# Inverse-root store and broadcast issued by GpSimd, and k^T v computed in two groups of head pairs per batch

## Chip, cores and metric

The kernel runs on one core of a Trainium2 chip. The metric is the device time of one execution in microseconds; the median of three runs is compared.

## What is computed

A linear attention without softmax, then two feed-forward blocks, all in float32 (reference, cut):

```python
kv  = np.einsum('bhsd,bhse->bhde', k, v)        # 8 batches, 8 heads, 576 rows, head size 64
out = np.einsum('bhsd,bhde->bhse', q, kv)
rms = np.sqrt(np.mean(out * out, axis=-1, keepdims=True) + 1e-06)
x   = (out / rms * g_norm)                       # then (4608, 512)
r   = np.maximum(x @ w_in, 0.0)                  # w_in 512 x 2048, w_out 2048 x 512
x   = (s * (r * r) + b) @ w_out
h   = x @ w2_in
out = (h * (1.0 / (1.0 + np.exp(-1.702 * h)))) @ w2_out
```

## The kernel before

**Tiling.** The 4608 tokens are nine token blocks of 512. A batch has 576 tokens, so block j holds the end of batch j-1 and the beginning of batch j. Activations lie transposed (features on partitions). A float32 product is made of three passes over a high and a low part of each operand, so one feed-forward step of 128 features takes twelve 128x128x512 matmuls. The first feed-forward of blocks 0 to 2 is plain (`plain`); later blocks are worked in pairs with seven products in place of eight (`first_products`, `second_plain`, `second_products`). During block 0 the weights of the first feed-forward are decoded from 64-bit words on the fly (`w_low`, `w_words`, `w_hi`, `w_lo`), a weight unit per step, by ScalarE and VectorE.

**What sets the order.** There is no scheduler: `at(slot, fn, ...)` enters a call with a slot number, the list is sorted by slot, and every engine's instructions are issued in that order. A slot is one step of twelve wide matmuls; block j of the plain stage begins at slot 32 j, so blocks 0 to 2 are slots 0 to 95. Each engine, and each queue that issues transfers, is in order: an instruction that waits holds back all behind it. SyncE (SP) issues all transfers, and each of its issues also waits for the one eight issues earlier to have landed (eight counting semaphores, used in turn). Buffers come from rings (`Slots`), 23 of 128x512 (`mid`), 42 twice as wide (`big`), 8 PSUM banks; a new tile waits for the last reader of the buffer that has been free longest.

**k^T v.** For each batch b, `kv_load` (L275) brings k and v of one head pair (two transfers of 256 KB), `tail_load` (L278, L280) the last 64 rows, `kv_product` (L311, L315) makes the 64x64 products of all four head pairs in one go (64 short passes and 8 tail passes), and `kv_keep` (L323) copies them to SBUF. The table `KV` gives the slot of the product for batches 1 to 7; the loads are entered 3.3 to 1.8 slots ahead, the tail 1.3 ahead. Batch 0 is done at the start, pair by pair.

**Attention of block j** (`attend`): q loads (L293), the products (L342), squares and copies, one mean over the heads (L396), then ln/exp and a Newton step (L369, L370) give the inverse root y for eight heads. `y_store` (L411) writes the eight rows of y to DRAM, `y_load` (L417) reads each row back broadcast to 64 partitions, two transfers per head pair, eight in all; `att_scale` (L422, VectorE) multiplies; `att_split` splits into high and low part, or from block 3 on stores to DRAM (`x0d`, L429). Both y steps stand on SP.

Of the kernel before, what the change touches and what calls it, by code (L numbers as in the profile page):

```python
# [10 lines left out]
AF = mybir.ActivationFunctionType  # L11
ALU = mybir.AluOpType

P = 128
T = 512
B, H, S, D = 8, 8, 576, 64
DM, DFF = 512, 2048
NP = H // 2
NG = NP // 2
# [6 lines left out]


START = [(-61, -60, -54, -52, -45), (-59, -54, -53, -47, -42), (-54, -48, -48, -43, -41), (-50, -49, -46, -40, -36)]
KV = (1, 29, 34, 64.6, 80, 86, 92)
CONV = [(0, 1, 2, 3), (-0.5, 0, 1, 1.5)]  # L30


# [31 lines left out]
def kernel(ctx: ExitStack, tc: tile.TileContext, q_h, kv_h, kt, vt, cst,  # L64
# [6 lines left out]
    nc = tc.nc  # L71
    pe, act, dve, pool = nc.tensor, nc.scalar, nc.vector, nc.gpsimd
# [13 lines left out]
    def drop(*tiles):  # L86
        for t in tiles:
            slots, n, _ = where.pop(id(t))
            slots.give(n)
# [4 lines left out]
    def new2(dtype, name):  # L94
        return new(mid, [P, T], dtype, name)

    def psum(name):
        return new(bank, [P, T], F32, name)
# [10 lines left out]
    kvs = [cp.tile([P, NG, 2, D], F32, name=f"kvs{i}") for i in range(4)]  # L109
# [158 lines left out]
    kvin, kvp, qin, xT, done = {}, {}, {}, {}, set()  # L268
    xd = [[dp.tile([NP, P, T], F32, name=f"x{m}d{j}") for j in range(NB)] for m in range(2)]
    yd = [dp.tile([H, T], F32, name=f"yd{j}") for j in range(NB)]  # L270
# [31 lines left out]
    def kv_product(b, units, first, last):  # L302
        if first:
            kvp[b] = psum("kv")
        kv = kvp[b].rearrange("q (g c) -> q g c", g=NP)
        for h in range(2):
            for c in range(4):
                for p in units:
                    r, o = p % 2 * D, c * P + h * D
                    kt_, vt_ = (t[:, o:o + D] for t in kvin[b, p])  # L310
                    pe.matmul(kv[r:r + D, p // 2, h * D:(h + 1) * D], lhsT=kt_, rhs=vt_, start=(p < 2 and h == 0 and c == 0), stop=False,  # L311
                              skip_group_check=True)
        for p in units:
            r = p % 2 * D
            pe.matmul(kv[r:r + D, p // 2, :], lhsT=tail_k[:, p // 2, p % 2, :], rhs=tail_v[:, p // 2, p % 2, :],  # L315
                      start=False, stop=True, skip_group_check=True)
            drop(*kvin.pop((b, p)))

    def kv_keep(b, p):
        r = p % 2 * D  # L320
        src = kvp[b].rearrange("q (g h c) -> q g h c", g=NP, h=2)
        if b:
            act.activation(kvs[b % 4], src[:, 0:NG], AF.Copy)  # L323
            done.update(("kv", b, n) for n in range(NP))
            drop(kvp.pop(b))
            return
        act.activation(kvs[0][r:r + D, p // 2], src[r:r + D, p // 2], AF.Copy)
        done.add(("kv", b, p))
        if p == NP - 1:
            drop(kvp.pop(b))  # L330
# [77 lines left out]

    def y_store(j):
        y = att.pop(j)  # L410
        nc.sync.dma_start(out=yd[j], in_=y[0:P:P // H])  # L411
        drop(y)

    def y_load(j, p):
        y = new2(F32, "yb")
        for h in range(2):
            nc.sync.dma_start(out=y[h * D:(h + 1) * D], in_=yd[j][2 * p + h:2 * p + h + 1].to_broadcast([D, T]))  # L417
        att[j, p] = (att[j, p][0], y)

    def att_scale(j, p):  # L420
# [312 lines left out]
    def at(slot, fn, *a):  # L733
        events.append((slot, len(events), fn, a))
# [11 lines left out]
    def attend(j, slot, gap, late):  # L746
        for g in range(NG):
            at(slot - 4 + g, q_load, j, g)
            at(slot + gap * g, att_product, j, (2 * g, 2 * g + 1))
            for r in range(2):  # L750
                at(slot + gap * g + 0.4 + 0.3 * r, att_square, j, 2 * g + r)
                at(slot + gap * g + 0.4 + 0.3 * r, att_copy, j, 2 * g + r)
        slot += gap + 1.4
        at(slot, block_mean, j)
        at(slot + 0.5, block_root, j)
        at(slot + 1.2, block_newton, j)
        at(slot + 1.8, y_store, j)
        for p in range(NP):
            at(slot + 2.7, y_load, j, p)
            at(slot + late + 1.1 * p, att_scale, j, p)  # L760
            at(slot + late + 1.1 * p + 0.3, att_split, j, p)

# [114 lines left out]
    for p in range(NP):  # L877
        at(-99 + p, kv_load, 0, p)
        if p == 0:
            at(-98.95, tail_load, 0)  # L880
        at(START[p][0], kv_product, 0, (p,), p == 0, p == NP - 1)
        at(START[p][0], kv_keep, 0, p)
        at(-98.9 + p, q_half, p)
        o, m, n, x = START[p][1:]
        attention((o, m, m, n, x), 0, p)
# [5 lines left out]
        weight(n - (5 if n < 12 else 4), n - 1, 1, CONV[1], 0, f, w)  # L891


    for b, slot in zip(range(1, B), KV):
        for p in range(NP):
            at(slot - 3.3 + 0.5 * p, kv_load, b, p)
        at(slot - 1.3, tail_load, b)
        at(slot, kv_product, b, range(NP), True, True)
        at(slot + 0.5, kv_keep, b, 0)


    for j in range(NPLAIN):
# [14 lines left out]
    for j, slot in zip(range(1, NPLAIN + 2), (10, 35.5, 49, 66)):  # L917
        attend(j, slot, 4, 4.8)
    for j in range(NPLAIN, NB - 2, 2):
        for n, slot in enumerate((5, 16) if j == NPLAIN else (0.5, 12)):  # L920
            attend(j + 2 + n, firsts[0, j] + slot, 4, 4.8)
# [14 lines left out]
    for k in range(2):  # L936
        slot = seconds[1, NB - 3] + 10 + 4 * k
# [10 lines left out]
    for i in range(NF // 2):  # L948
        slot = 50 + 5.4 * i
# [10 lines left out]
    slot = 32 * NPLAIN + 4  # L960
# [64 lines left out]
```

## Time and profile before

| | us |
|---|---|
| median of three runs | 1581.72 (1580.92 to 1583.14) |
| the profiled execution's own time | 1583.73 |
| its span in the trace | 1581.9 |
| TensorE (PE) busy | 1538.5 (97%) |
| VectorE (DVE) busy | 1063.5 (67%) |
| ScalarE (ACT) busy | 793.4 (50%) |
| GpSimd (POOL) busy | 1.6 (12 instructions) |
| transfers, share of 16 DMA engines | 70.3% |

Times are counted from the start of the span. The shares are averages over stages with different limits: the start (to about 37 us), block 0 with the decoding of weights (to about 143), blocks 1 and 2 (to about 360), and then the paired blocks. TensorE's busy time grows when its granted clock falls, so a busy PE is not always PE at its full rate. A row of a timeline gives start, duration, engine, line, operation, and in brackets the idle time before it with what ended that.

### The profile page before, as it was taken

The page shows a single profiled execution, that of the slowest core. Times are in us where ns is not written, and L with a number is a line of the kernel's source. Part 1 is how long each engine was busy: PE and PEld are TensorE (multiplying, and loading weights), DVE is VectorE, ACT ScalarE, POOL GpSimd, SP SyncE. Part 2 cuts the span into 40 slices and gives each one's busy share as a digit, 9 for nine tenths or more (in the row PEclk, how much of TensorE's full clock was granted, in tenths as well). Part 3 has the DMA queues.
Part 4 walks back from the last instruction along what each step waited for, and adds up shares of the span by engine and source line. Part 5 has one row for each costly group of instructions (what it writes and reads, how often), then busy time and mean ns, then how long its engine had stood idle before and what let it go on. Part 6 is the DMA issues. An engine that isn't in the chain of part 4 may idle for free.

```text
span 1581.9 us, 20440 instructions
## 1 busy us (share of the span) xinstructions
PE 1538.5 (97%) x7316; PEld 1238.8 (78%) x7316; DVE 1063.5 (67%) x1535; ACT 793.4 (50%) x1162; POOL 1.6 (0%) x12
## 2 busy tenths in 40 slices
PE   7988998999899999999999999999999999999999
PEld 4766776787688877888888888888888888888887
DVE  4996463565679477866672579867967796688422
ACT  4987453454598357944692225423532452234222
POOL 0000000000000000000000000000000000000000
PEclk8999999999999999999999999999999999999999
DMA  9535547779899688959870866885788478746680
GB/s 303 190 121 187 202 160 283 259 266 319 267 333 336 214 316 334 379 187 339 332 297 16 303 223 239 273 300 199 264 287 301 171 271 281 259 139 206 223 311 27
DMA packets 177444, 392.09 MB, mean 248 GB/s; under 512 B 22912, under 2 KB 54656, under 8 KB 177344
## 3 DMA queue, kind: packets, MB, share of 16 engines
q1 hardware_dynamic: 177344, 390.80, 70.3%
q8 instruction: 58, 0.95, 0.2%
q14 instruction: 42, 0.34, 0.1%
HBM read 300.42 MB, written 90.31 MB: 247 GB/s over the span
## 4 chain that ended last, share of the span: by engine, by line
PE 84%; DMA 6%; DVE 5%; ACT 2%; SPq 1%; issue 1%; DVEq 0%; ACTq 0%
PE o L523 25%; PE o L694 19%; PE d L566 9%; PE a L566 9%; PE h L480 7%; PE b L566 4%; PE f L566 4%; PE c L566 4%; DMA v_in<-in_kv 2%; DMA raw<-in_w_in 2%; DVE cu L157 1%; PE o_ps L342 1%; PE kv L311 1%; DVE ca L158 1%; DMA x0d<-oc 1%
## 5 line engine op out<-in xcount | busy, mean ns | idle before, releaser
L523 PE MATMUL o<-gh,w 128*128 128x512 f32 x1280 | 407.3, 391 | 2.0 <-DVE w L173 0.8
L523 PEld LDWEIGHTS o<-gh,w 128*128 128x128 f32 x1280 | 239.8, 188 | 59.4 <-DVE w L173 3.6
L694 PE MATMUL o<-gh,wl 128*128 128x512 f32 x896 | 276.4, 389 | 0.0
L523 PE MATMUL o<-gl,w 128*128 128x512 f32 x640 | 249.9, 391 | 0.4 <-DVE gl L513 0.2
L694 PEld LDWEIGHTS o<-gh,wl 128*128 128x128 f32 x896 | 168.2, 188 | 34.9
L480 PE MATMUL h<-xh,w 128*128 128x512 f32 x512 | 171.9, 397 | 7.0 <-DVE w L173 3.3
L694 PE MATMUL o<-gl,wl 128*128 128x512 f32 x448 | 174.3, 389 | 0.0
L566 PE MATMUL d<-xh,wl 128*128 128x512 f32 x448 | 157.9, 393 | 5.7 <-DVE r L592 5.7
L566 PE MATMUL a<-xh,wl 128*128 128x512 f32 x448 | 157.6, 393 | 1.0 <-DMA wl<-wsd 1.0
L523 PEld LDWEIGHTS o<-gl,w 128*128 128x128 f32 x640 | 120.3, 188 | 26.9 <-DVE gl L513 2.4
L480 PEld LDWEIGHTS h<-xh,w 128*128 128x128 f32 x512 | 96.6, 190 | 35.6 <-DVE w L173 6.8
L582 ACT ACTIVATE c<-a 128x512 f32<-128x512 f32 x56 | 33.5, 597 | 168.0 <-PE a L566 165.0
L566 PEld LDWEIGHTS d<-xh,wl 128*128 128x128 f32 x448 | 84.6, 189 | 25.9 <-DVE r L592 7.4
L566 PEld LDWEIGHTS a<-xh,wl 128*128 128x128 f32 x448 | 84.6, 189 | 21.9 <-issue 1.9
L480 PE MATMUL h<-xl,w 128*128 128x512 f32 x256 | 100.7, 393 | 0.2 <-DVE xl L442 0.2
L694 PEld LDWEIGHTS o<-gl,wl 128*128 128x128 f32 x448 | 84.1, 188 | 17.5
L637 DVE TENSOR_TENSOR gl<-r,gh 128x512 fp32r<-128x512 f32 x96 | 65.1, 687 | 40.5 <-PE o L523 23.4
L566 PE MATMUL d<-xl,wl 128*128 128x512 f32 x224 | 87.6, 391 | 0.0
L566 PE MATMUL a<-xl,wl 128*128 128x512 f32 x224 | 87.6, 391 | 0.0
L668 ACT ACTIVATE gh<-t 128x1024 fp32r<-128x1024 f32 x48 | 51.0, 1062 | 72.5 <-DVE t L659 60.6
L621 ACT ACTIVATE r<-r 128x1024 f32<-128x1024 f32 x84 | 84.6, 1054 | 0.0
L673 DVE TENSOR_TENSOR gl<-r,gh 128x1024 fp32r<-128x1024 f32 x64 | 77.1, 1218 | 6.9 <-ACT gh L668 6.9
(114 smaller groups left out, 2483.7 us busy)
## 6 DMA issues: line engine op xcount, KB each, us to landing
wl<-wsd SPq DMA_DIRECT2D x168, 512.0 KB, 6.7
wl<-wo2S SPq DMA_DIRECT2D x64, 512.0 KB, 5.4
wsd<-op SPq DMA_DIRECT2D x96, 256.0 KB, 4.1
w<-wod SPq DMA_DIRECT2D x48, 512.0 KB, 7.8
wl<-wo2A SPq DMA_DIRECT2D x48, 512.0 KB, 4.6
raw<-in_w_in SPq DMA_DIRECT2D x32, 512.0 KB, 7.1
raw<-in_w_out SPq DMA_DIRECT2D x32, 512.0 KB, 8.6
wl<-wsd SPq DMA_DIRECT2D x56, 256.0 KB, 5.8
```

The costliest lines, as they stand in the source:

```text
L157: dve.scalar_tensor_tensor(out=t, in0=raw[:, :, 1], scalar=SIGN_TOP, in1=t, op0=ALU.bitwise_and, op1=ALU.bitwise_or)
L158: dve.tensor_tensor(out=q, in0=t, in1=q, op=ALU.add)
L311: pe.matmul(kv[r:r + D, p // 2, h * D:(h + 1) * D], lhsT=kt_, rhs=vt_, start=(p < 2 and h == 0 and c == 0), stop=False, skip_group_check=True)
L480: pe.matmul(h, lhsT=a, rhs=b, start=(n == 0), stop=(n == 3 * NP - 1))
L523: pe.matmul(acc[m, j][c], lhsT=a, rhs=x, start=(f == 0 and n == 0), stop=(f == NF - 1 and n == 2))
L566: pe.matmul(o, lhsT=a, rhs=b, start=(first and n == 0), stop=(n == 5), skip_group_check=not first)
L582: act.activation(st["c1"], st[0], AF.Copy)
L621: act.activation(R[q, n], R[q, n], fn)
L637: dve.tensor_sub(out=gl, in0=R[q, i][:, half, :], in1=gh.bitcast(F32))
L668: act.activation(hi, src, AF.Copy)
L673: dve.tensor_sub(out=lo, in0=src, in1=hi.bitcast(F32))
L694: pe.matmul(so[k, d], lhsT=a, rhs=b, start=(first and n == 0 and i == 0 and e == 0), stop=(n == 3 and i == 1 and e == 2), skip_group_check ...
```

## The change

`y_store` and `y_load` are issued by GpSimd. The eight transfers of `y_load` are entered from 2.6 slots after the mean's slot on, pair by pair 0.9 slots apart, where all stood at 2.7. The products of k and v are made in two groups of two head pairs, each with a slot of its own; a group's loads are entered 5.5 and 4.8 slots ahead, the tail 4 slots ahead of the first group. The accumulation's first-write flag is set per group, and each group is copied to SBUF by itself, so the copy is half as wide and there are two per batch. One PSUM bank holds a batch's products from its first group to its second.

```diff
-KV = (1, 29, 34, 64.6, 80, 86, 92)
+KV = ((1, 5), (20, 27), (34, 41), (46, 57), (62.5, 66.5), (74, 79), (84, 89))
...
+        opens = units[0] if b else 0
...
-                    pe.matmul(kv[r:r + D, p // 2, h * D:(h + 1) * D], lhsT=kt_, rhs=vt_, start=(p < 2 and h == 0 and c == 0), stop=False,
+                    pe.matmul(kv[r:r + D, p // 2, h * D:(h + 1) * D], lhsT=kt_, rhs=vt_, start=(p in (opens, opens + 1) and h == 0 and c == 0), stop=False,
...
-            act.activation(kvs[b % 4], src[:, 0:NG], AF.Copy)
-            done.update(("kv", b, n) for n in range(NP))
+            act.activation(kvs[b % 4][:, p // 2], src[:, p // 2], AF.Copy)
+            done.update((("kv", b, p), ("kv", b, p + 1)))
...
     def y_store(j):
         y = att.pop(j)
-        nc.sync.dma_start(out=yd[j], in_=y[0:P:P // H])
+        pool.dma_start(out=yd[j], in_=y[0:P:P // H])
...
-            nc.sync.dma_start(out=y[h * D:(h + 1) * D], in_=yd[j][2 * p + h:2 * p + h + 1].to_broadcast([D, T]))
+            pool.dma_start(out=y[h * D:(h + 1) * D], in_=yd[j][2 * p + h:2 * p + h + 1].to_broadcast([D, T]))
...
-            at(slot + 2.7, y_load, j, p)
+            at(slot + 2.6 + 0.9 * p, y_load, j, p)
...
-    for b, slot in zip(range(1, B), KV):
-        for p in range(NP):
-            at(slot - 3.3 + 0.5 * p, kv_load, b, p)
-        at(slot - 1.3, tail_load, b)
-        at(slot, kv_product, b, range(NP), True, True)
-        at(slot + 0.5, kv_keep, b, 0)
+    for b, slots in zip(range(1, B), KV):
+        for g, slot in enumerate(slots):
+            for r in range(2):
+                at(slot - 5.5 + 0.7 * r, kv_load, b, 2 * g + r)
+            if g == 0:
+                at(slot - 4, tail_load, b)
+            at(slot, kv_product, b, (2 * g, 2 * g + 1), True, True)
+            at(slot + 0.6, kv_keep, b, 2 * g)
```

Three places in the order of instructions. From L304 on the changed kernel's line numbers are one higher.

SP in block 0, around the y store of block 1 (`raw` are weight units, `yd` and `yb` the store and the broadcast of y), before:

```order
L138 DMA raw_1003<-in_w1_out 128x1024
L411 DMA yd1_139<-y_949 8x512
L133 DMA raw_1035<-in_w1_in 128x4x256
L417 DMA yb_1037<-yd1_139 64x512 x2
L417 DMA yb_1040<-yd1_139 64x512 x2
L417 DMA yb_1043<-yd1_139 64x512 x2
L417 DMA yb_1046<-yd1_139 64x512 x2
L138 DMA raw_1075<-in_w1_out 128x1024
```

and with the change:

```order
L133 DMA raw_888<-in_w1_in 128x4x256
L275 DMA k_in_909<-in_kv 128x512
L275 DMA v_in_910<-in_kv 128x512
L138 DMA raw_938<-in_w1_out 128x1024
L275 DMA k_in_945<-in_kv 128x512
L275 DMA v_in_946<-in_kv 128x512
L133 DMA raw_983<-in_w1_in 128x4x256
L278 DMA tail_k_78<-in_kt 128x256
L280 DMA tail_v_79<-in_vt 64x4x64 x2
L138 DMA raw_1016<-in_w1_out 128x1024
L133 DMA raw_1048<-in_w1_in 128x4x256
```

The store and the eight broadcasts left SP, and the loads of batch 2's first group came in at about the same place.

TensorE around the product of batch 4, before:

```order
L480 MATMUL h<-xl,w 128x512
L480 MATMUL h<-xh,w 128x512
L311 MATMUL kv<-v_in,k_in 64x64 x32
L315 MATMUL kv<-tail_v,tail_k 64x128 x4
L523 MATMUL o<-gh,w 128x512
```

and the second group of batch 4 with the change (the first stands 11 slots ahead of it, and both ahead of that place):

```order
L481 MATMUL h<-xh,w 128x512
L312 MATMUL kv<-v_in,k_in 64x64 x16
L316 MATMUL kv<-tail_v,tail_k 64x128 x2
L524 MATMUL o<-gh,w 128x512
L524 MATMUL o<-gl,w 128x512
```

The run of short matmuls is halved and stands in two places.

SP in the paired stage, around the broadcast of block 5 (`wl` are weights for TensorE, `x0d` the store of the scaled block), before:

```order
L417 DMA yb<-yd_143 64x512 x8
L243 DMA wsd_0_104<-op 128x512 x2
L254 DMA wl<-wsd_4_100 128x1024
L254 DMA wl<-wsd_4_100 128x512
L254 DMA wl<-wsd_5_101 128x1024
L429 DMA x0d_125<-oc 128x512
```

and with the change:

```order
L293 DMA qq<-in_q 128x128
L243 DMA wsd_0_104<-op 128x512 x2
L254 DMA wl<-wsd_4_100 128x1024
L254 DMA wl<-wsd_4_100 128x512
L254 DMA wl<-wsd_5_101 128x1024
L430 DMA x0d_125<-oc 128x512
```

The eight broadcasts ahead of the weight loads are gone from SP; they stand on GpSimd's queue, which holds nothing else after its first memsets.

## Rows read from the trace of the kernel before

**Rows 1.** The page's head.

```profile
span 1581.9 us, 20440 instructions
```

**Rows 2.** TensorE's waits, whole span: total us, times, longest us.

```profile
PE kv L311 <- DMA v_in<-in_kv: 12.5, 8, 2.6
PE d L566 <- DVE r L592: 5.7, 4, 2.9
...
PE h L480 <- DVE w L173: 3.3, 2, 2.0
...
PE a L566 <- DMA wl<-wsd: 1.0, 1, 1.0
```

**Rows 3.** Stretches around products: length, PE, PEld, DVE, ACT, POOL, PEclk, DMA, GB/s.

```profile
243.80:256.50 12.70, 4.91 (x74) 4.25 (x73) 3.73 (x6) 2.42 (x4) 0.00 (x0) 0.73 0.97 339
303.90:311.30 7.40, 4.09 (x74) 3.48 (x73) 0.15 (x1) 0.00 (x0) 0.00 (x0) 0.84 0.92 295
328.30:332.30 4.00, 2.86 (x74) 2.52 (x73) 0.00 (x0) 0.00 (x0) 0.00 (x0) 1.00 1.06 378
...
135.55:138.10 2.55, 2.55 (x74) 2.38 (x73) 2.45 (x6) 2.52 (x5) 0.00 (x0) 1.00 0.02 6
```

**Rows 4.** Chain of waits after batch 2's product: start, us, what.

```profile
138.08 2.99 PE h L480 x12
141.06 2.72 PE o L523 x12
```

**Rows 5.** SP's issues ahead of batch 4's product.

```profile
225.04 4.94 SPq L417 DMA_DIRECT2D yb<-yd  x8
...
246.52 0.44 SPq L275 DMA_DIRECT2D v_in<-in_kv  x1
```

**Rows 6.** Stages in block 0 and block 2, columns as in Rows 3.

```profile
60.00:80.00 20.00, 19.60 (x105) 13.44 (x104) 19.32 (x35) 18.50 (x33) 0.00 (x0) 1.00 0.46 166
...
300.00:350.00 50.00, 45.55 (x346) 37.39 (x346) 26.20 (x41) 21.40 (x32) 0.00 (x0) 0.97 0.85 293
```

**Rows 7.** VectorE's timeline in block 0.

```profile
96.75 0.69 DVE L370 SCALAR_TENSOR_TENSOR y<-y,y 128x512 f32<-128x512 f32 x1
...
109.38 0.75 DVE L422 SCALAR_TENSOR_TENSOR oc<-oc,g_col,yb 128x512 f32<-128x512 f32 x1
...
124.47 0.74 DVE L422 SCALAR_TENSOR_TENSOR oc<-oc,g_col,yb 128x512 f32<-128x512 f32 x1
...
135.19 0.68 DVE L173 TENSOR_TENSOR w<-ca,w 128x512 fp32r<-128x512 f32 x1
```

**Rows 8.** SP's issues around the broadcast of block 5.

```profile
398.32 0.60 SPq L411 DMA_DIRECT2D yd<-y  x1
...
402.39 6.34 SPq L417 DMA_DIRECT2D yb<-yd  x8
...
409.88 1.67 SPq L254 DMA_DIRECT2D wl<-wsd  x3
411.65 0.38 SPq L429 DMA_DIRECT2D x0d<-oc  x1
```

**Rows 9.** Chain of waits behind that.

```profile
422.20 2.92 PE d L566 x6
425.12 2.56 PE a L566 x6
```

**Rows 10.** Line L417, all 64 broadcasts: issue ns min/median/max, and landing.

```profile
L417 SPq DMA_DIRECT2D yb<-yd x64: 444/587/1253, 99.3 to 615.5; - x64
...
DMA to landing us min/median/max: 2.8/3.1/6.0
```

**Rows 11.** ScalarE's copy of one batch's products: duration ns min/median/max.

```profile
L323 ACT ACTIVATE kvs<-kv x7: 368/385/387, 46.0 to 351.4; 128x256 f32<-128x256 f32 x7
```

**Rows 12.** VectorE's groups from 97 to 125 us: busy us, mean ns.

```profile
L173 DVE TENSOR_TENSOR w<-ca,w 128x512 fp32r<-128x512 f32 x7 | 4.8, 682 | 0.0
L152 DVE TENSOR_SCALAR cu<-cu 128x512 uint32<-128x512 uint32 x7 | 3.0, 427 | 0.2
```

## The prediction

> **What bounds it now.** I read the head of the page first: the span is 1581.9 us [rows 1], the profiled execution took 1583.73, the median of the runs is 1581.72. So the sum below is made against 1583.73, and 2.0 us come off at the end. TensorE is busy 97% of the span (the table above), so the change can gain only where TensorE waits, or where its granted clock is low because it has just waited.
>
> Then TensorE's waits [rows 2]. The largest that the change touches is `kv` on `v_in`: 12.5 us in 8 waits, 2.6 at the longest. The reader is to see that one batch's product waits several times, once for each head pair whose load is late. `d` on `r` (5.7) and `h` on the weight word `w` (3.3) come next; `a` on `wl` is a single 1.0.
>
> Then the stretches around single products [rows 3]. The product of batch 2 is the undisturbed one: 2.55 us for its 74 matmuls, clock 1.00. Batch 4's took 12.70 us at a granted clock of 0.73, batch 5's 7.40 at 0.84, batch 6's 4.00 at 1.00. In these three the transfers were busy at 0.97, 0.92 and 1.06 of the 16 engines, against 0.02 in the first. So the loads, entered only 3.3 slots ahead, compete with the rest and are late. For batch 4 something else adds: the issues on SP. The eight broadcasts of y took SP 4.94 us from 225.04 on, and the last `v_in` went out at 246.52, after the product had begun to wait [rows 5].
>
> Then block 0. There DVE is busy 19.32 us of 20 and TensorE 19.60 [rows 6]: weights are decoded as they are used, and DVE sets the pace. TensorE's wait for `w` [rows 2] belongs here.
>
> Last, the broadcast of block 5 [rows 8]: eight issues from 402.39 for 6.34 us, the three loads of `wl` at 409.88 and the store `x0d` at 411.65, behind them on the same queue. The chain that ended last then shows six `d` in 2.92 us and six `a` in 2.56 [rows 9], where twelve matmuls at full clock take 2.72 [rows 4], so six take 1.36.
>
> **The change part by part.**
>
> *Loads ahead, two groups (batches 4, 5, 6).* Undisturbed, three products are 3 x 2.55 = 7.65 us; they took 12.70 + 7.40 + 4.00 = 24.10 [rows 3]. At most 16.45 us are to be had. A slot is twelve matmuls, 2.72 us, so 5.5 slots are 15 us, against 9 before; a group needs two pairs (1 MB) in place of four; and the eight broadcasts are not ahead of the loads on SP any more. I take the whole. Against that, a product is a run of small matmuls, and the twelve matmuls after batch 2's took 2.99 us, against 2.72 later [rows 4]: 0.27 us for each break. Five batches (3 to 7) are broken once more each: 1.35 us. **-16.45 + 1.35 = -15.1.** Bounds: -17 (the breaks cost nothing), and -8 if half of the loads stay late.
>
> *Batch 2.* Its product moves from slot 29 to 20 and 27, and the copy with it. At 135.55 it stood just ahead of a wait: `w` was ready at 135.19 + 0.68 = 135.87 [rows 7], and the next `h` began at 138.08 [rows 4]. So 2.2 us of the 2.55 were TensorE's own delay there; at the new slots the product lies in waits that TensorE has anyway, because DVE sets the pace. **-2**, bounds 0 and -2.8 (2.55 + 0.27).
>
> *SP without y (block 5).* The 6.34 us leave SP ahead of `wl` and `x0d`. Gone with them: the wait of `a` on `wl`, 1.0; one of `d` on `r`, 2.9, since the late `x0d` holds a buffer for which DVE waits, and DVE's `r` behind it [rows 2]; the slow clock after them, (2.92 - 1.36) + (2.56 - 1.36) = 2.76 [rows 4, 9]. Together 6.7; that the `x0d` store is behind the wait of `d` I infer from the order alone, so I take **-5**, bounds 0 and -6.7. The Trainium skill speaks against this term ("DMA: Bandwidth & Descriptors", section "Issuing engines are not separate DMA queues"): all issuers share the same 16 engines, and a second issuer saves only the time of issuing, usually small beside the transfer. By that rule the sum would be 5 us poorer; here the issuing itself is 6.34 us [rows 8], so I go by the row.
>
> In block 0 SP's freedom brings nothing: DVE sets the pace [rows 6], and word loads that go out sooner wait for it.
>
> *The copies.* One more `kvs` copy per batch on ScalarE, at most 0.385 us each [rows 11], and half as wide; seven are 2.7 at most. Most lie beside TensorE's work; three fall in block 0, where ScalarE is at 18.50 of 20 [rows 6]. **+0.5**, bounds 0 and 1.2.
>
> *The price X of an issue by GpSimd.* No row of before shows one. The nearest are SP's issues of the same transfers: 0.44 us shortest, 0.587 median, 1.25 longest; landing 2.8 to 6.0 us, median 3.1 [rows 10]. GpSimd can be cheaper than SP's shortest or dearer than its longest; nothing excludes either. I take X = 1.25, the dear end. GpSimd holds nothing else, so what queues behind its waits is only y itself. Who waits is DVE's `att_scale`. In block 0, y is done at 96.75 + 0.69 = 97.44 [rows 7]; store issue and landing 1.25 + 3.1, first pair 2.5 + 3.1: ready at 107.4, while its scale began at 109.38 [rows 7]; each later pair comes 2.5 us after, and the last scale began at 124.47 against 114.9. So it hides. In the paired stage DVE has room. **+0.5** for a scale that comes a little late there, bounds 0 and (rival below) much more.
>
> *Sum:* -15.1 - 2 - 5 + 0.5 + 0.5 = -21.1. 1583.73 - 21.1 = 1562.6 for a profiled execution, less 2.0: **1560** for the median, rounded down from 1560.6.
>
> **Rivals.**
>
> *The loads stay late in part.* The stretches already show 0.92 to 1.06 of the transfers' capacity [rows 3], and a load entered sooner only stands sooner in a full queue; it may also wait on SP for a buffer. Against it: over 300 to 350 the share is 0.85 [rows 6], so there is room outside the bursts. Half of the first term gone (+7.5), and half of the third (+2.5), leaves -11: **1571**.
>
> *GpSimd's issues are slow, and the scale waits: slower.* DVE is in order, so an `att_scale` that waits for `yb` holds all decoding behind it, in the stage where DVE sets the pace. Pair p is there at 97.44 + X + 3.1 + 2X(p+1) + 3.1. At X = 4 the first is there at 115.6 (109.38 is needed) and the last at 139.6 (124.47 is needed): 15 us late, all of it in the time. In the four paired-stage broadcasts up to block 8 the same lateness of 15 us reaches TensorE by half, as DVE has slack there: some 30. With -21 that is +24: **1606**. It decides from X = 3.1: there the last pair of block 0 is 7 us late and half of 7 at the four others makes 14, together the 21 gained. What speaks for it: DVE's units here take 427 ns and 682 ns for tiles of one size [rows 12], so some run in a faster form, and DVE leaves no gap [rows 6]. Against it: no row shows GpSimd issuing. The Trainium skill has a rule by which it would go this way ("SBUF — State Buffer", section "SBUF: two separate sides"): transfers issued by GpSimd need descriptors that it writes through a port shared with DVE, and DVE's fast forms lock it out. The page's figure is 620 ns alone and some 3100 beside a copy by DVE; by that estimate the gain would be just about eaten (1582).
>
> *It does nothing that can be told.* A measurement of this kernel tells some 0.2%, 3.2 us, from no change. Gain and lateness would have to cancel within that: X close to 3.1 with the loads in time.
>
> **How the numbers follow.** The forecast has 0.62. Late loads 0.23: the full queues are in the rows, the room beside them too. Slow issues 0.12: a fast form of DVE is in the rows, but between two of its instructions GpSimd can get in. Nothing 0.03. Faster by over 0.2% is the forecast and the late loads: 0.85; same 0.03; slower 0.12. The range: all upper bounds together (-17 - 2.8 - 6.7) give 1583.73 - 2.0 - 26.5 = 1555, a little less if waits that I haven't named go too, so 1551; above, late loads with 5 us of new waits, or an X between 2 and 3, 1576. Some 0.18 lies outside.
>
> **What would show it.** In the changed profile TensorE should no longer wait for `v_in`; each group of a product should take about 1.3 us at a clock of 1.00; the waits of `a` and `d` near block 5's broadcast should be gone, with its six matmuls at 1.36; the `yb` transfers should land ahead of every `att_scale` of block 0. The second group of batch 2 should no longer hold back an `h` whose `w` is ready. I am wrong if DVE's scale waits for `yb` in block 0 or if the landing of `yb` on GpSimd's queue takes over 6 us (slow issues); if `kv` still waits for `v_in` or `k_in` with the transfers at 0.9 or more (late loads); or if the waits that go are made up by others, on `r` or on `wl`, in the paired stage.

## The result, and the profile after

The changed kernel takes **1565.2 us** (median of four runs, 1564.6 to 1566.29) against 1582.43 for the kernel before beside it: ratio 0.9891, 95% interval 0.9874 to 0.9908, so 17.2 us less. The forecast was 1560, which is 21.7 less than the 1581.72 it started from. The profiled executions differ by 19.1 us: that of before was 1.3 above its median here, that of the change 0.6 below. Medians and ratios below leave out one execution of one kernel (number 11), which took 3108.3 us.

One sentence ahead of the prediction is to be corrected: a batch's products don't hold one PSUM bank from the first group to the second. Each group takes a bank of its own and gives it back with its copy (`first` is true for both, and `kv_keep` drops the bank each time). No step of the prediction rests on it.

The page's head, and TensorE's waits in the changed kernel (total us, times, longest), which answer to [rows 1, 2]:

```profile
span 1562.8 us, 20560 instructions
```

```profile
PE d L567 <- DVE r L593: 7.0, 6, 2.0
...
PE kv L312 <- DMA v_in<-in_kv: 2.3, 2, 1.2
...
PE h L481 <- DVE w L173: 0.4, 1, 0.4
```

(`a` and `d` are matmuls of the paired blocks; `d` reads `r`, which VectorE writes.) `v_in` went from 12.5 to 2.3, and what is left lies in the start, where batch 0 is worked as before (1.5 of the 12.5 lay there). The wait for `w` went from 3.3 to 0.4, that of `a` on `wl` is gone. The wait of `d` on `r` rose from 5.7 to 7.0. A group of a product, with the wide matmuls at its edges (the two groups of batch 5, columns as in [rows 3]), now reads:

```profile
239.03:240.57 1.54, 1.54 (x38) 1.37 (x38) 0.96 (x2) 1.51 (x3) 0.00 (x0) 1.00 0.91 311
252.47:254.00 1.53, 1.53 (x41) 1.36 (x38) 0.78 (x2) 1.41 (x3) 0.00 (x0) 1.00 1.07 415
```

The clock is at 1.00 beside transfers at 0.91 and 1.07: here full transfers don't slow a product whose operands are there. The whole batch takes 3.07 us, where it took 7.40.

The step of twelve matmuls behind a group is slower, as it was behind one piece. Here are the steps ahead of and behind the first of these groups, and, before the change, those ahead of and behind batch 7's one piece:

```profile
236.38 2.72 PE h L481 x12
...
240.40 2.95 PE o L524 x12
```

```profile
346.14 2.72 PE h L480 x12
...
351.31 2.99 PE o L523 x12
```

From the end of the step ahead to the end of the step behind, less 2.72 us for that step, a group costs 1.53 us and one piece 2.72.

Where the time went is read from the chain that ended last, at the same matmuls (start, us, what). Before:

```profile
143.78 2.72 PE h L480 x12
...
359.74 1.36 PE a L566 x6
...
457.77 87.04 PE o L523 x384
...
631.18 87.32 PE o L523 x384
```

and in the changed kernel:

```profile
141.20 2.72 PE h L481 x12
...
341.57 1.36 PE a L567 x6
...
436.82 87.06 PE o L524 x384
...
611.81 87.04 PE o L524 x384
```

| stretch | gained, us | sum so far | forecast |
|---|---|---|---|
| start and block 0 | 2.6 | 2.6 | 2 |
| blocks 1 and 2 (batches 3 to 7) | 15.6 | 18.2 | 15.1 |
| first paired blocks, broadcasts of blocks 5 and 6 | 2.8 | 21.0 | 5 |
| next pair, broadcasts of blocks 7 and 8 | -1.6 | 19.4 | 0 |

After 632 us (612) the two run alike. So the products gave what was forecast; the paired blocks gave 1.2 us where 5, less 0.5 for lateness, were forecast. The reason stands in VectorE's timeline of the changed kernel, at the first scale of blocks 5 and 7 (in brackets the idle time before, and what ended it):

```profile
391.14 0.75 DVE L423 SCALAR_TENSOR_TENSOR oc<-oc,g_col,yb 128x512 f32<-128x512 f32 x1 [2.73 <-DMA yb<-yd]
...
560.98 0.75 DVE L423 SCALAR_TENSOR_TENSOR oc<-oc,g_col,yb 128x512 f32<-128x512 f32 x1 [3.08 <-DMA yb<-yd]
```

VectorE stands at the first scale until the broadcast has landed. At block 5 it did so before the change too, and then for `x0d` as well (at block 7 it waited 0.48):

```profile
408.74 0.75 DVE L422 SCALAR_TENSOR_TENSOR oc<-oc,g_col,yb 128x512 f32<-128x512 f32 x1 [2.17 <-DMA yb<-yd]
...
418.79 0.69 DVE L585 TENSOR_TENSOR u<-b,c 128x512 f32<-128x512 f32 x1 [2.66 <-DMA x0d<-oc]
```

In the changed kernel TensorE then waits at `d`:

```profile
401.84 0.50 PE L567 MATMUL d<-xh,wl 128*128 128x512 f32 x1 [2.04 <-DVE r L593]
...
568.24 0.50 PE L567 MATMUL d<-xh,wl 128*128 128x512 f32 x1 [1.81 <-DVE r L593]
```

The issue is not at fault. The lines of the store and of the broadcast on GpSimd (duration ns min/median/max; then time to landing, us):

```profile
L412 POOL DMA_DIRECT2D yd<-y x8: 565/566/740, 96.8 to 588.0; - x8
...
DMA to landing us min/median/max: 1.7/4.5/5.6
```

```profile
L418 POOL DMA_DIRECT2D yb<-yd x64: 518/526/723, 99.2 to 597.1; - x64
...
DMA to landing us min/median/max: 2.7/3.7/7.2
```

X, the price of an issue, is 0.53 us, cheaper than SP's 0.587 [rows 10]. What is late in the paired blocks is the landing of the store. The broadcasts of blocks 5 to 8 land after 4.3, 3.3, 3.8 and 3.0 us (medians), and did so after 4.2, 3.1, 5.5 and 2.8 before.

Nine of GpSimd's 72 issues are longer than the others, 0.607 to 0.740 us against 0.568 at most. During each of the nine a TENSOR_SCALAR of VectorE begins, during the other 63 only twice. The store of block 6 is one of the nine, that of block 7 is not:

```profile
418.07 0.74 POOL L412 DMA_DIRECT2D yd<-y  x1 [27.90 <-DVE y L371]
...
549.83 0.56 POOL L412 DMA_DIRECT2D yd<-y  x1 [122.53 <-DVE y L371]
```

```profile
418.30 0.42 DVE L151 TENSOR_SCALAR cu<-cu 128x512 f32<-128x512 f32 x1
```

That is at most 0.2 us an issue. It isn't what makes the store late: block 7's store, issued in 0.56 us, is the slowest to land (5.6).

### The profile page after: what moved, and what is told of

The parts are those of the page before. It is cut to its first block, busy times and chain, and to the rows that moved or that the text cites. A ratio compares the mean times of both kernels' runs of the same rounds, so it can differ in the third digit from the quotient of the medians.

```text
span 1562.8 us, 20560 instructions
## 1 busy us (share of the span) xinstructions
PE 1533.9 (98%) x7316; PEld 1235.5 (79%) x7316; DVE 1063.9 (68%) x1535; ACT 795.4 (51%) x1169; POOL 40.3 (3%) x84
## 4 chain that ended last, share of the span: by engine, by line
PE 84%; DVE 7%; issue 3%; DMA 3%; ACT 3%; SPq 0%; POOL 0%; DVEq 0%; ACTq 0%; POOLq 0%
PE o L524 26%; PE o L695 19%; PE h L481 8%; PE d L567 8%; PE a L567 8%; PE b L567 4%; PE f L567 4%; PE c L567 4%; DVE cu L157 1%; DVE w L173 1%; DMA yb<-yd 1%; PE kv L312 1%; DMA qq<-in_q 1%; PE o_ps L343 1%; DVE ca L158 1%
```

## The experiments

Ratios are to the kernel before, run beside each on the same chip.

| kernel | us | ratio, 95% interval |
|---|---|---|
| changed | 1565.2 | 0.9891 (0.9874 to 0.9908) |
| 1: y on GpSimd alone | 1583.6 | 1.0006 (0.9995 to 1.0017) |
| 2: k^T v alone | 1564.01 | 0.9880 (0.9861 to 0.9898) |
| 3: changed, store on SP | 1561.93 | 0.9867 (0.9852 to 0.9883) |
| 4: changed, SP held | 1562.76 | 0.9870 (0.9852 to 0.9888) |
| 5: 1 and the lead alone | 1571.06 | 0.9936 (0.9924 to 0.9949) |
| 6: changed, old lead | 1575.52 | 0.9964 (0.9950 to 0.9978) |
| 7: changed, batch 2 back | 1568.31 | 0.9922 (0.9909 to 0.9935) |
| 8: 3, scale later | 1557.75 | 0.9855 (0.9840 to 0.9870) |
| 9: 2, scale later | 1560.8 | 0.9859 (0.9840 to 0.9879) |
| 10: changed, scale later | 1559.01 | 0.9852 (0.9827 to 0.9876) |
| 11: changed, old lead but for the tail | 1571.83 | 0.9929 (0.9916 to 0.9941) |

**1 and 2: the two halves of the change.** Number 1 is the kernel before with the new `y_store` and `y_load`; number 2 is the changed kernel with

```diff
-        pool.dma_start(out=yd[j], in_=y[0:P:P // H])
+        nc.sync.dma_start(out=yd[j], in_=y[0:P:P // H])
-            pool.dma_start(out=y[h * D:(h + 1) * D], in_=yd[j][2 * p + h:2 * p + h + 1].to_broadcast([D, T]))
+            nc.sync.dma_start(out=y[h * D:(h + 1) * D], in_=yd[j][2 * p + h:2 * p + h + 1].to_broadcast([D, T]))
-            at(slot + 2.6 + 0.9 * p, y_load, j, p)
+            at(slot + 2.7, y_load, j, p)
```

> The kernel before with the y store and broadcast on GpSimd (and the 0.9-slot spacing); the table of k^T v stays as it was. My theory (the gain is that of k^T v's earlier, halved loads; y off SP is worth 3.5 us at block 5's broadcast, and gives 2 to 3 back because y then lands later): batch 4's product gains about 5 us, since the eight issues of 4.94 us leave SP ahead of its last load; batches 5 and 6 keep their waits; together about -6, 1576 us (1573 to 1579). Rival (k^T v was late because y's issues and SP's wait for y stood in its way): nearly the whole gain appears here, 1568 or less.

> The changed kernel with y's store and broadcast back on SP, all at slot 2.7 behind the mean's as before; k^T v in two groups, 5.5 slots ahead, as changed. My theory: TensorE's waits for v_in are as small as in the changed kernel (under 4 us in total), block 5's late wl and x0d are back (+3.5), the late broadcast in the other paired blocks is gone (-2): 1565 to 1568 us. Rival (SP had to be freed): v_in's waits stay at 8 us or more, 1574 or more.

Number 1 gained nothing, less than both theories said; number 2 gained all, and is a little faster than I expected. Waits in number 1:

```profile
PE kv L311 <- DMA v_in<-in_kv: 14.3, 10, 3.6
PE d L566 <- DVE r L592: 8.9, 6, 2.8
...
DVE oc L422 <- DMA yb<-yd: 8.7, 3, 4.0
```

and in number 2:

```profile
PE d L567 <- DVE r L593: 5.7, 4, 3.0
...
PE kv L312 <- DMA v_in<-in_kv: 1.1, 2, 0.6
```

With y off SP and the old loads, `v_in` waits as long as ever: SP's issues were not what made the loads late. Against the matmuls of before, number 1's TensorE is 0.4 us ahead as block 5's broadcast begins, 6.7 once it is over, 4.2 at the end of block 6's, and 0.5 behind after block 7's. So freeing SP did gain at block 5, more than I had summed, and blocks 6 and 7, where VectorE waits 3.1 and 4.0 us for the late `yb`, gave all of it back.

**3 and 4: why y lands late.** Number 3 is the changed kernel with the store alone on SP:

```diff
-        pool.dma_start(out=yd[j], in_=y[0:P:P // H])
+        nc.sync.dma_start(out=yd[j], in_=y[0:P:P // H])
```

Number 4 only adds a second, unused store by SP:

```diff
     def y_store(j):
         y = att.pop(j)
+        nc.sync.dma_start(out=yd2[j], in_=y[0:P:P // H])
         pool.dma_start(out=yd[j], in_=y[0:P:P // H])
```

> The changed kernel with the y store alone back on SP; the broadcast stays on GpSimd. My theory (in the paired blocks the store lands after 4.3 to 5.6 us instead of 1.8 because SP, no longer held by its wait for y, keeps the transfer engines full while y goes out): with the store on SP, SP waits for y again, its transfers run dry, the store lands in about 2 us, VectorE's scale waits under 3 us in total (7.8 in the changed kernel), and the waits of d on r fall from 7.0 to about 4: 1 to 3 us faster than the changed kernel, 1562 to 1564. Rival (the lateness is the broadcast's own, through GpSimd): store early, scale still waits 6 us or more, no gain.

> The changed kernel, in which SP also stores y once more to a second place in DRAM, just ahead of GpSimd's own store; GpSimd's store and broadcast stay the ones that are used. So SP is held until y is ready, as before the change, and only that. My theory (full transfers make GpSimd's store late): GpSimd's store lands in 2.5 us or less in the paired blocks too, where it took 4.3 to 5.6. Rival (a store issued by GpSimd is itself slow beside a busy VectorE): it still takes 4 us or more there. Time: within 3 us of the changed kernel under both, as SP's hold costs and the earlier y gains.

In number 4 GpSimd's store landed after 1.8, 5.1, 1.7 and 3.3 us in blocks 5 to 8: early in two of the four, where all four were late in the changed kernel (4.7, 4.8, 5.6, 4.7). I had expected all four early. SP had issued nothing for 5.3, 1.0, 4.4 and 3.0 us ahead of its own store there, so the two early stores are those behind the longest holds. The stretches from issue to landing tell the stores apart (columns as in [rows 3]). In the changed kernel, first the store made during block 0, then that of block 7:

```profile
96.77:98.60 1.83, 1.83 (x9) 1.50 (x8) 1.73 (x4) 1.53 (x3) 0.70 (x1) 1.00 0.30 114
...
549.83:555.40 5.57, 5.57 (x26) 4.63 (x25) 3.72 (x7) 5.57 (x8) 0.56 (x1) 1.00 1.02 376
```

in number 4, blocks 5 to 8:

```profile
379.85:381.60 1.75, 1.75 (x10) 1.44 (x9) 1.00 (x2) 1.75 (x4) 0.56 (x1) 1.00 0.30 107
415.16:420.20 5.04, 5.04 (x24) 4.18 (x23) 4.21 (x9) 4.62 (x7) 0.74 (x1) 1.00 1.05 415
551.00:552.70 1.70, 1.70 (x9) 1.43 (x8) 0.69 (x1) 1.70 (x3) 0.56 (x1) 1.00 0.23 41
588.76:592.00 3.24, 2.20 (x11) 1.51 (x10) 3.17 (x7) 1.23 (x2) 0.60 (x1) 1.00 0.93 314
```

and before, on SP, blocks 7 and 8:

```profile
570.45:572.60 2.15, 2.15 (x11) 1.77 (x10) 0.81 (x2) 2.15 (x3) 0.00 (x0) 1.00 0.21 30
...
606.57:611.10 4.53, 3.50 (x16) 2.59 (x15) 4.39 (x9) 1.23 (x2) 0.00 (x0) 1.00 0.75 291
```

GpSimd's store lands in under 2 us where the transfers are at 0.2 to 0.3, and takes 3.3 to 5.6 where they are at 0.9 and more; the rows of before are from SP's store to its first broadcast. They show that SP's own store was not always quick: with the transfers at 0.75 it took 4.5. VectorE's share goes the other way: in block 0 it is busy for 1.73 of 1.83 us, and the store is quick. Where SP had waited long in its order for y, the transfers had run dry; freed, it keeps them full while y goes out. An early store alone did not help VectorE: in number 4 its waits for `yb` are 10.1 us in all (7.8 in the changed kernel), and those of `d` for `r` 8.3 (7.0).

Number 3's time came as expected, but not by the way expected: VectorE's waits for `yb` rose to 10.0, and `d`'s for `r` stayed, at 7.4. The broadcast went out 2.6, 2.3 and 3.1 us behind the store in blocks 5, 7 and 8 (5.2 in block 6; 5.1 to 6.4 in the changed kernel). It then landed later, after 7.4, 4.6, 8.0 and 7.6 us in blocks 5 to 8, with the transfers at 0.90 to 0.99. Half of the gain to the changed kernel's profile (1.2 of 2.2 us) is there at TensorE's first matmuls, which the edit doesn't touch, and the intervals overlap. So number 4 shows what makes the store late, and number 3 that an early store moves the lateness to the broadcast; that either is faster than the changed kernel they don't show.

**5, 6 and 11: lead or halves.** Number 5 is number 1 with

```diff
-            at(slot - 3.3 + 0.5 * p, kv_load, b, p)
-        at(slot - 1.3, tail_load, b)
+            at(slot - 5.5 + 0.7 * p, kv_load, b, p)
+        at(slot - 4, tail_load, b)
```

Number 6 is the changed kernel with the old lead; number 11 has the first of its two lines alone:

```diff
-                at(slot - 5.5 + 0.7 * r, kv_load, b, 2 * g + r)
+                at(slot - 3.3 + 0.5 * r, kv_load, b, 2 * g + r)
-                at(slot - 4, tail_load, b)
+                at(slot - 1.3, tail_load, b)
```

> The kernel with y on GpSimd alone (the first experiment), plus k^T v's loads entered 5.5 to 3.4 slots ahead in place of 3.3 to 1.8, the tail 4 ahead; the product stays one piece at the slots of the kernel before. My theory (the loads were entered too late): the waits for v_in fall below 3 us from 14.3, so about 12 to 15 us faster than the first experiment's 1583.6: 1569 to 1572 us. Rival (four pairs in one burst don't come through transfers at 0.92 to 1.06, however early they are entered; it was halving and spreading that helped): v_in still waits 7 us or more, 1576 or more.

> The changed kernel with the lead put back: a group's loads 3.3 and 2.8 slots ahead, the tail 1.3; the halves and their slots stay as changed. My theory (lead): v_in's waits come back in part, 4 to 9 us against 2.3, and the time is 3 to 8 us above the changed kernel: 1568 to 1573. Rival (halving and spreading): v_in's waits stay under 3 us, 1564 to 1566.

> The changed kernel with a group's loads of k and v 3.3 and 2.8 slots ahead as in the sixth experiment, but the tail 4 slots ahead as changed. In the sixth, v_in waited only 0.8 us and the tail 4.3. Theory now (in halves, k and v come in time even 3.3 slots ahead; what the sixth lost was the tail): v_in's waits under 2 us, the tail's under 0.5, 1565 to 1568 us. Rival (the k and v loads need the longer lead also in halves; the tail's wait only hid theirs): v_in waits 4 us or more, 1570 or more.

Waits of the products in number 5, in number 6, in number 11:

```profile
PE kv L311 <- DMA v_in<-in_kv: 4.4, 4, 1.5
```

```profile
PE kv L316 <- DMA tail_v<-in_vt: 4.3, 2, 3.0
...
PE kv L312 <- DMA v_in<-in_kv: 0.8, 1, 0.8
```

```profile
PE kv L312 <- DMA v_in<-in_kv: 3.1, 5, 1.2
```

Against number 1, by the ratios, the lead alone gave 0.70% (11 us), halves and new slots alone 0.42% (7 us), both together 1.15% (18 us). As totals they add up, but not where the loads act. Over blocks 1 and 2, at the same matmuls of the profiled executions, the lead alone gains 13.6 us on number 1, halves and new slots 7.7, both 15.4: they take away in part the same waits. The paired blocks, where number 6 loses 3.6 us on number 1 and the changed kernel gains 1.9, hide it in the totals. Number 5 came in the time expected; of its 4.4 us of waits 1.6 lie in the start. Number 6's wait was for the tail, not for `v_in` as I had expected, and its time is above both ranges. With the tail early (number 11) 0.35% comes back. `v_in` waits 3.1 there, between the figures of the two theories (1.2 of it after the start), and the time is the rival's. The remaining 0.38% (6 us) to the changed kernel is the lead of k and v; its profiled execution shows 2.2 of them in blocks 1 and 2.

**7: batch 2.** Its two groups go back to where the one product stood:

```diff
-KV = ((1, 5), (20, 27), (34, 41), (46, 57), (62.5, 66.5), (74, 79), (84, 89))
+KV = ((1, 5), (28, 29), (34, 41), (46, 57), (62.5, 66.5), (74, 79), (84, 89))
```

> The changed kernel with batch 2's two groups at slots 28 and 29 in place of 20 and 27 (one slot apart, so that the first is copied before the second). My theory (at 29 a product stands where TensorE would not have waited, at 20 and 27 it hides in waits for VectorE's weight words): from some 150 us on, TensorE is 2 to 3 us later than in the changed kernel, and the time 1567 to 1568. Rival (VectorE alone sets block 0's end, wherever the product stands): TensorE's place at 150 us differs by under 0.7 us, 1565.

3.1 us slower by the medians, 4.9 by the ratios. The wait for `w` is back, and the step of twelve matmuls that began at 141.20 in the changed kernel begins at 145.09. That is 3.9 later, but 1.2 of it is there at 32 us, ahead of all that the edit moves, so 2.7 are the edit's, as expected:

```profile
PE h L481 <- DVE w L173: 2.9, 2, 1.9
```

```profile
145.09 2.72 PE h L481 x12
```

**8, 9 and 10: the scale later.** One number, on numbers 3, 2 and the changed kernel:

```diff
-            attend(j + 2 + n, firsts[0, j] + slot, 4, 4.8)
+            attend(j + 2 + n, firsts[0, j] + slot, 4, 6.3)
```

> The kernel with the y store on SP and the broadcast on GpSimd (the third experiment, 1561.9 us), with the scale and the store of the scaled block 1.5 slots (4.1 us) later in blocks 5 to 8, behind the mean's slot by 6.3 in place of 4.8. My theory (VectorE, in order, stands at the first scale until the broadcast has landed, and TensorE then waits for d's r): VectorE's waits for yb in these blocks fall to under 1 us (about 7 there), d's waits for r fall from 7.4 to about 4, 2 to 4 us gained: 1558 to 1560. Rival (d waits for r because VectorE is simply full there): r's waits stay within 1 us of 7.4, no gain.

> k^T v as changed, y's store and broadcast both on SP (the second experiment, 1564.0 us), with the scale and the store of the scaled block 1.5 slots later in blocks 5 to 8. My theory (with y on SP, the broadcast lands early, and what is lost at block 5 is SP's eight issues ahead of wl and x0d, which a later scale doesn't move): about 1 us gained, 1562 to 1564. Rival (the late scale is worth the same wherever y is issued): 1558 to 1560.

> The changed kernel (1565.2 us, y all on GpSimd), with the scale and the store of the scaled block 1.5 slots later in blocks 5 to 8, and nothing else. My theory (what y on GpSimd gives back is VectorE standing at a scale whose broadcast is late): VectorE's waits for yb there fall from 7 to under 2 us, d's waits for r from 7.0 to about 3.5, 1559 to 1562 us. Rival (the store on SP was needed for it): 1564 or more.

Waits in number 10:

```profile
PE d L567 <- DVE r L593: 3.2, 4, 1.3
...
DVE oc L423 <- DMA yb<-yd: 4.6, 4, 2.0
```

Numbers 8 and 10 came as expected in time and in `d`'s wait (3.2 in both); number 10 still waits 4.6 us for `yb`, more than expected. By the ratios the later scale gains 6.2 us on the changed kernel, 1.9 on number 3 and 3.3 on number 2, and each pair of intervals overlaps. At the same matmuls of the profiled executions it gains 6.0, 5.1 and 3.7 us in the paired blocks, at `d` and the matmuls just behind it. Number 9's time lies between the two ranges, nearer to the rival's, and so shows my theory too narrow: the later scale also gains with y on SP (`d`'s wait 5.7 to 2.8). What the three have in common is the scale's place in VectorE's order, and by the ratios they can't be told apart. All three ratios lie below that of the changed kernel; only number 8's interval is clear of it.

## Why the prediction was right, and where a term was off

- **Loads ahead, two groups: right.** Forecast -15.1, measured 15.6 over blocks 1 and 2. Number 2, with y on SP, gains the same 15.6 there. The price of the second break was about right. A group costs 1.53 us with the slower step behind it, two 3.06, and one piece 2.72: some 0.3 for the second break, forecast 0.27. Numbers 1 and 2 show that this half of the change is the whole gain, number 5 that full transfers did not keep early loads from coming in time, and number 2 that SP's issues did not. That I also let the broadcasts leaving SP count for batch 4 is not borne out: number 2 has them on SP, and `v_in` waits 1.1.
- **Batch 2: right, somewhat small.** Forecast -2; the start and block 0 show 2.6, number 7 2.7 at the matmuls.
- **The copies: not seen.** Forecast +0.5. ScalarE makes 14 copies of 0.278 us where it made 7 of 0.385, and after the start TensorE waits for none.
- **SP without y, block 5: mis-sized.** Forecast -5. The wait on `wl` went as said. That of `d` on `r` (2.9) did not go with the late `x0d`: VectorE's wait for `x0d` (2.66) is gone, but its wait for `yb`, which was 2.17 before, is 2.73, and `d` still waits 2.04. TensorE's place moved 3.5 us at that broadcast and fell back to 2.8 by the end of block 6's. Number 10, which moves the scale and the `x0d` store behind it, brings that wait down to 0.4. The Trainium skill's rule ("DMA: Bandwidth & Descriptors", section "Issuing engines are not separate DMA queues": a second issuer saves only the time of issuing) would have given nothing here. By number 1's total (ratio 1.0006) it is borne out, though not by its steps: 6 us were gained at block 5 and spent at blocks 6 and 7.
- **The price X: mis-sized, in the wrong place.** I took 1.25 us; it is 0.53. The cost that I put at 0.5 us was in the landing: I had carried over 3.1 us, the broadcast's median, for the store too, which takes 4.7 to 5.6 in the paired blocks of the changed kernel. "In the paired stage DVE has room" was the step that failed: there the first scale waits 2.7, 1.4 and 3.1 us in blocks 5 to 7, and blocks 7 and 8 lose 1.6. The trace of before already spoke against it, with 2.17 us at block 5.
- **Rivals.** Slow issues did not come: no issue of the changed kernel took more than 0.74 us. The Trainium skill has a rule for it ("SBUF — State Buffer", section "SBUF: two separate sides": GpSimd writes descriptors through a port that VectorE's fast forms lock). The nine longer issues above agree with it, if TENSOR_SCALAR, 0.42 us where other operations on the same tile take 0.68, is such a fast form. But the cost here is at most 0.2 us an issue, far from the estimate in the prediction. Where VectorE was busiest, in block 0, the store was among the quickest to land (1.8 us). The rival's mechanism, a scale that waits for y, did come, at a small part of its price and from another cause. Late loads did not come. With the scale later (number 10, 1559.01) the time stands where the forecast had it.
- **Signs of being wrong.** Two came, in part. The waits that went were made up in the paired stage: `d`'s for `r` rose from 5.7 to 7.0. And a broadcast did take over 6 us to land (7.2, block 2's, with the transfers at 0.96), but no scale of block 0 waited for it.

What stays open: why numbers 3 and 4 are a little faster than the changed kernel, if they are, and how late the scale can be put. Neither was tried further.

## To carry to other kernels

When a product waits for its operands, enter the loads earlier and in smaller bursts, and put the pieces where their engine waits for something else anyway; here the lead alone gave 11 us, the halves in their new slots alone 7, and in blocks 1 and 2 both took away in part the same waits. Moving a latency-bound round trip to a queue of its own did not make it faster here: by waiting, the old queue had let the transfers run dry, and the freed queue fills them. Before moving it, look whether its reader can simply stand later in its engine's order, which cost one number here and gained 4 to 6 us at the same matmuls (2 to 6 by the ratios).

## What was not expected of the hardware

A 16 KB store to DRAM on an otherwise empty queue landed in 1.7 to 1.8 us while the transfers were at 0.2 to 0.3, and in 3.3 to 5.6 at 0.9 and above: a queue of its own gave it no precedence. GpSimd's issue of a broadcast, 0.53 us, is no dearer than SP's 0.587, and steadier: 0.518 to 0.723 against 0.444 to 1.253. The longer issues coincide with a TENSOR_SCALAR of VectorE that begins meanwhile, and are longer by at most 0.2 us.
